# Expert layer in 512-token pairs, attention in 32-column tiles, and a written-out step order in a linear-attention and expert kernel

## The chip, the core and the metric

One core of a Trainium2 chip. TensorE multiplies matrices, VectorE and ScalarE do element-wise work, GpSimd (POOL) does little here, and SyncE (SP) issues the transfers. Times are microseconds on the device. The metric is the time of one execution of the whole program; three runs are given, and one more execution was profiled.

## The reference, cut to what matters

```python
# q, k, v, a_re, a_im: (4 batches, 8 heads, 768 steps, 48)
mag = sqrt(a_re**2 + a_im**2);  a = (a_re, a_im) * min(mag, 0.999) / (mag + 1e-6)
for t in range(768):
    S_re, S_im = a_t * S  (complex) + outer(k_t, v_t) on the real part
    y_t = q_t @ S_re
x = y as 3072 tokens of 384            # 8 heads x 48
h = x @ w_in                           # 384 -> 2048
g = h * sigmoid(1.702 * h)
out = g @ w_out                        # 2048 -> 384
```

All data are float32. The recurrence is computed in blocks of 128 steps: running products of magnitudes and running sums of angles scale and rotate q and k, so that inside a block a masked product of q and k stands for the recurrence, and a 96-row state carries it from block to block. Each head has a cosine and a sine part, 2 x 48 rows.

## The kernel before, in words

**Units.** The 3072 tokens are cut into 12 units of T = 256 tokens, three to a batch, and each unit has two halves of 128. A unit passes through three stages.

*Preparation* (`prepare_part`, L512 to L644): the coefficients are loaded into `ri`, ScalarE takes squares, logarithms, exponentials, an arctangent and sines, VectorE multiplies, and runs three kinds of scan (L570, L586, L604) over 3 x 256 columns. Six buffers `s0` to `s5` hold what is between, and their roles rotate from unit to unit. q and k are scaled and rotated in `qk` and `qr` and then copied by SP (`remap`, L646) into `qkh`, head by head: the cosine part in rows 0 to 47, the sine part in rows 64 to 111, the gaps being zero from memsets at the start (L384 to L386). Unit 0 is prepared in two halves.

*Attention* (`attend`, L657): for each half and each group of four heads, `scores` (L690) multiplies k by q into the PSUM bank `p_ps` in column tiles 64 wide, VectorE multiplies by the mask into `pm` (L694), `mix` (L716) adds masked scores times v and the state times q into `x_ps` in tiles 32 wide, `turn` (L736) transposes k of 112 rows into the bank `k_ps`, ScalarE copies it to `kt` (L747), `zed` (L743) multiplies it by v into `z_ps` in tiles of 48 columns, and VectorE adds it to the state `st` (L752). ScalarE rounds `x_ps` into `xhi` (L724), VectorE puts the rest into `xlo` (L728).

*Expert layer* (`moe`, L761): for each of 8 blocks of 256 hidden columns, `hidden` (L782) multiplies weights by the unit's 256 tokens into one of two banks `h_ps`, ScalarE writes Silu in float32 into `g32` (L794), VectorE rounds it into `gh` (L796) and puts the rest into `gl` (L797), and `project` (L812) multiplies slices of `gh` and `gl` (128 tokens wide, stationary) by 384 columns of output weights (moving) into two banks `o_ps`. Each product of float32 values is three products of rounded ones: high by high, high by low, low by high. VectorE copies `o_ps` to `osb` (L823) and SP stores it (L826). Unit 0 uses whole float32 weights and activations, which takes TensorE two passes a matmul, because the split of the weights is not done yet. So a unit of 256 tokens has 144 hidden matmuls of 256 columns and 96 output matmuls of 384; unit 0 has 48 and 32.

**Weights** come as 64-bit words, are converted (`convert`, L446: L462 on ScalarE, L463, L466, L469 on VectorE) and split into high and low (`split`, L471), 16 pieces of each. `inspect` and `sign` read weights and coefficients again and reduce them (L839, L858); `decide` (L862) turns the result into a flag, and at the end the program takes a general path (`general`, L890) if the data were out of range, which they are not here. The opening matmuls (L637) come before the first scores.

**Order.** Every step is added to a `Plan` (L82) with its engine, an estimated duration, a rank, and what it reads and writes. `Plan.order` (L291) plays the steps forward and backward with these durations, 160 rounds for each of five settings, and keeps the order with the lowest estimated cost; the rank comes from `prep_rank`, `attn_rank`, `moe_rank` and so on (L1075 to L1096). The steps are issued in this order, so each engine's stream is fixed, and an engine waits at the first instruction that is not ready. SP's queue is one of these streams. ScalarE loads a set of functions (L999) where a step needs another one than the last.

Of the kernel before, what the change touches and what calls it, by code (L numbers as in the profile page):

```python
# [10 lines left out]
F32 = mybir.dt.float32  # L11
# [10 lines left out]
P = 128  # L22
L = 128
HL = 64
# [11 lines left out]
KD = 112  # L36
UPB = 3
TWO_PI = 6.2831845
# [18 lines left out]
class Clock:  # L57


    def __init__(self):  # L60
        self.now, self.done, self.full = -1, 0.0, False

    def end(self, start, dur, work):
        t = start
        while dur > 1e-6:
            k = int(t / WINDOW + 1e-9)
            if k != self.now:
                self.full = k == self.now + 1 and self.done >= BUSY
                self.now, self.done = k, 0.0
            rate = 1.0 if self.full else 0.5  # L70
            step = min(dur, ((k + 1) * WINDOW - t) * rate)
            self.done += step * work
            dur -= step
            t += step / rate
        return t


def lag(a, b):
    return LAG if b != "PE" else 0.0 if a == b else LAG_PE


class Plan:  # L82
# [5 lines left out]
    def add(self, eng, dur, rank, fn, r=(), w=(), tab=None, name="", grp=None, work=1.0):  # L88
# [9 lines left out]
        self.ops.append((eng, dur, rank, fn, deps, tab, name, grp, work))  # L98

    def link(self):  # L100
        self.after = [[] for _ in self.ops]
        for n, o in enumerate(self.ops):
            for d in o[4]:
                self.after[d].append(n)

    def groups(self):
        todo = {}
        for o in self.ops:
            if o[7] is not None:
                todo[o[7]] = todo.get(o[7], 0) + 1  # L110
        return todo

    def forward(self, rank):

        ops, after = self.ops, self.after
        left = [len(o[4]) for o in ops]
        ready = [0.0] * len(ops)
        free = dict(FREE)
        wait = {e: [] for e in ENGINES}
        can = {e: [] for e in ENGINES}  # L120
        table, hw, dma, idle = None, 0.0, 0.0, 0.7
        todo, held = self.groups(), None
        clock = Clock()
        for n, k in enumerate(left):
            if not k:
                heapq.heappush(wait[ops[n][0]], (0.0, n))
        start = [0.0] * len(ops)
        done = 0
        while done < len(ops):
            best = None  # L130
            for e in ENGINES:
                while wait[e] and wait[e][0][0] <= free[e]:
                    n = heapq.heappop(wait[e])[1]
                    heapq.heappush(can[e], (rank[n], n))
                if can[e]:
                    s = free[e]
                elif wait[e]:
                    s = wait[e][0][0]
                else:
                    continue  # L140
                if best is None or s < best[0]:
                    best = (s, e)
            s, e = best
            if not can[e]:
                while wait[e] and wait[e][0][0] <= s:
                    n = heapq.heappop(wait[e])[1]
                    heapq.heappush(can[e], (rank[n], n))
            if e == "ACT":
                fit = [x for x in can[e] if ops[x[1]][5] in (None, table) or held in (None, ops[x[1]][7])]
                if not fit:  # L150
                    later = [free[x] for x in ENGINES if x != e and free[x] > s]
                    later += [wait[e][0][0]] if wait[e] else []
# [1009 lines left out]
```

## Time and profile before

| what | value |
|---|---|
| median of three runs | 596.96 us (594.47 to 601.34) |
| the profiled execution, whole | 595.74 us |
| its span, first to last instruction | 594.3 us |
| granted TensorE clock, mean | 0.996 of full speed |
| TensorE / VectorE / ScalarE busy | 557.5 / 472.4 / 272.1 us |
| HBM read / written | 53.87 / 4.72 MB |

The span is the profiled execution without what lies around its first and last instruction, 1.44 us. A busy engine has an instruction in work; matmuls are pipelined, so the distance between their starts tells their price, and not the length of one.

### The profile page before, as it was taken

How to read it: one execution, taken by the hardware profiler on the slowest of the kernel's cores; microseconds unless marked ns; L12 is line 12 of the kernel's file. 1: busy time of each engine (PE TensorE's matmuls, PEld its weight loads, DVE VectorE, ACT ScalarE, POOL GpSimd, SP SyncE). 2: the span in 40 equal slices, each digit the busy share in tenths (PEclk: the TensorE clock that was granted, in tenths of full speed). 3: DMA queues.
4: the chain of work that ended last, by engine and by line, in shares of the span. 5: the costliest groups of instructions: out<-in, count | busy, mean ns of one | idle time of the engine just before them, and what ended most of it. 6: DMA issues, size and time to landing. Idle time of an engine off the chain costs nothing.

```text
span 594.3 us, 13835 instructions
## 1 busy us (share of the span) xinstructions
PE 557.5 (94%) x5804; PEld 512.9 (86%) x5804; DVE 472.4 (79%) x827; ACT 272.1 (46%) x373; POOL 23.8 (4%) x75
## 2 busy tenths in 40 slices
PE   0489999999999999899999999999899999999995
PEld 0377778999989999899999899999889999999994
DVE  7999999989879788788789697798689779554433
ACT  8878477247463552742732723532552642111110
POOL 5110000000010000000000000000000000000000
PEclk9999999999999999999999999999999999999998
DMA  8478962363651830833807825743851832722211
GB/s 344 143 257 333 236 191 70 73 143 129 108 168 32 175 120 14 163 108 84 191 33 130 230 80 110 174 149 92 156 185 47 205 93 64 168 73 58 68 43 41
DMA packets 31526, 78.48 MB, mean 132 GB/s; under 512 B 4448, under 2 KB 9568, under 8 KB 31456
## 3 DMA queue, kind: packets, MB, share of 16 engines
q1 hardware_dynamic: 31456, 77.52, 48.6%
q8 instruction: 47, 0.77, 0.6%
q14 instruction: 23, 0.19, 0.1%
HBM read 53.87 MB, written 4.72 MB: 99 GB/s over the span
## 4 chain that ended last, share of the span: by engine, by line
PE 86%; DMA 4%; ACT 3%; DVE 3%; SPq 1%; issue 0%; ACTq 0%
PE o_ps L812 34%; PE h_ps L782 33%; PE x_ps L716 7%; PE p_ps L690 6%; PE z_ps L743 3%; PE k_ps L736 3%; DMA qkh<-qk 2%; DMA raw<-in_w_out_dram 1%; PE h_ps L637 1%; DMA raw_w<-in_w_in_dram 1%; DVE qk L444 1%; DMA ri<-in_a_dram 1%; DVE pm L694 1%; ACT L999 0%; ACT raw L462 0%; DVE s L604 0%
## 5 line engine op out<-in xcount | busy, mean ns | idle before, releaser
L782 PE MATMUL h_ps<-xhi,hiA 128*128 128x256 f32 x528 | 152.0, 288 | 0.0
L782 PE MATMUL h_ps<-xlo,hiA 128*128 128x256 f32 x528 | 149.0, 282 | 0.0
L782 PE MATMUL h_ps<-xhi,loA 128*128 128x256 f32 x528 | 149.0, 282 | 0.0
L794 ACT ACTIVATE g<-h_ps 128x512 f32<-128x512 f32 x88 | 52.7, 598 | 173.5 <-PE h_ps L782 99.6
L782 PEld LDWEIGHTS h_ps<-xhi,hiA 128*128 128x128 f32 x528 | 100.2, 190 | 2.4 <-issue 1.2
L782 PEld LDWEIGHTS h_ps<-xlo,hiA 128*128 128x128 f32 x528 | 100.3, 190 | 0.3
L782 PEld LDWEIGHTS h_ps<-xhi,loA 128*128 128x128 f32 x528 | 100.5, 190 | 0.0
L812 PE MATMUL o_ps<-hiU,gh 128*128 128x384 f32 x352 | 93.9, 347 | 0.0
L812 PE MATMUL o_ps<-loU,gh 128*128 128x384 f32 x352 | 89.7, 335 | 0.0
L812 PE MATMUL o_ps<-hiU,gl 128*128 128x384 f32 x352 | 89.6, 335 | 0.0
L812 PEld LDWEIGHTS o_ps<-loU,gh 128*128 128x128 f32 x352 | 63.7, 188 | 0.0
L812 PEld LDWEIGHTS o_ps<-hiU,gl 128*128 128x128 f32 x352 | 63.6, 188 | 0.0
L797 DVE TENSOR_TENSOR gl<-g,gh 128x512 fp32r<-128x512 f32 x88 | 60.4, 687 | 3.7
L796 DVE CAST gh<-g 128x512 fp32r<-128x512 f32 x88 | 36.9, 419 | 31.3 <-ACT g L794 21.1
L812 PEld LDWEIGHTS o_ps<-hiU,gh 128*128 128x128 f32 x352 | 57.6, 190 | 3.9 <-issue 2.6
L839 DVE TENSOR_REDUCE fit<-raw_w 128x1 f32<-128x256 f32 x96 | 37.6, 411 | 19.1 <-DMA raw_w<-in_w_in_dram 9.7
L690 PEld LDWEIGHTS p_ps<-qkh 128*64 128x64 f32 x768 | 36.9, 136 | 13.7 <-issue 4.6
L694 DVE TENSOR_TENSOR pm<-p_ps,mask 128x512 f32<-128x512 f32 x48 | 32.9, 686 | 19.7 <-PE p_ps L690 19.4
L690 PE MATMUL p_ps<-qkh 128*64 128x128 f32 (+1 forms) x768 | 43.6, 253 | 4.5 <-DMA qkh<-qk 2.6
L444 DVE TENSOR_TENSOR qk<-qk,s 128x768 f32<-128x768 f32 (+1 forms) x52 | 45.6, 889 | 2.5 <-ACT s L630 2.2
L999 ACT ACT_TABLE_LOAD x36 | 46.2, 1283 | 1.4 <-PEq L1150 0.8
L747 ACT ACTIVATE kt<-k_ps 128x448 f32<-128x448 f32 x40 | 21.7, 543 | 41.4 <-PE k_ps L736 25.5
(94 smaller groups left out, 763.8 us busy)
## 6 DMA issues: line engine op xcount, KB each, us to landing
v<-in_v_dram SPq DMA_DIRECT2D x24, 352.0 KB, 3.8
ri<-in_a_dram SPq DMA_DIRECT2D x11, 768.0 KB, 5.2
qk<-in_qk_dram SPq DMA_DIRECT2D x11, 768.0 KB, 4.9
qkh<-qr SPq DMA_DIRECT2D x22, 288.6 KB, 5.9
qkh<-qk SPq DMA_DIRECT2D x22, 288.6 KB, 6.5
raw<-in_w_in_dram SPq DMA_DIRECT2D x8, 768.0 KB, 7.3
raw<-in_w_out_dram SPq DMA_DIRECT2D x8, 768.0 KB, 6.6
raw_w<-in_w_in_dram SPq DMA_DIRECT2D x24, 256.0 KB, 2.8
```

The costliest lines, as they stand in the source:

```text
L444: add(en, t, rank, lambda: e.tensor_tensor(out=out, in0=a, in1=b, op=alu), **kw)
L690: mm(p_ps[to : to + HL, j, lo:L], lhsT=at(h, 1, c)[:, lo : lo + HL], rhs=at(h, 0, c)[:, lo:L], start=True, stop=True)
L694: add("DVE", d_t(CW), rk(4 * c + hh), lambda hh=hh: dve.tensor_tensor(out=pm[hh].rearrange("p (a b) t -> p a b t", b=2), in0=p_ps.rearrang ...
L716: mm(x_ps[32 * j : 32 * j + 32, r, :], lhsT=lt, rhs=rt, start=n == 0, stop=n == len(steps) - 1)
L747: add("ACT", a_t(4 * KD) - 0.12, rk(4 * c + hh), lambda: act(out=kt[0][:, :, 0:KD], in_=k_ps[:, :, 0:KD], func=AF.Copy), r=["K"], w=["kt"])
L782: mm(h_ps[hb][:, f, :], lhsT=ww[:, r * T + f * P : r * T + (f + 1) * P], rhs=x[:, r, :], start=n == 0, stop=n == last)
L794: add("ACT", a_t(CW) - 0.15, rk(i), lambda hb=hb: act(out=g32, in_=h_ps[hb], func=AF.Silu, scale=SLOPE), r=[f"h{hb}"], w=["g"], tab=SILU, ...
L796: add("DVE", d_t(CW, 2), rk(i), lambda gb=gb: dve.tensor_copy(out=high.g(gb), in_=g32), r=["g"], w=[f"gh{gb}"])
L797: add("DVE", d_t(CW), rk(i), lambda gb=gb: dve.tensor_tensor(out=glo[gb], in0=g32, in1=high.g(gb).bitcast(F32), op=ALU.subtract), r=["g", ...
L812: mm(o_ps[t], lhsT=x[:, f, t * L : (t + 1) * L], rhs=y[:, f * DM : (f + 1) * DM], start=i == 0 and f == 0 and n == 0, stop=i == NP - 1 and ...
L839: add("DVE", d_t(CK), rk + 2, lambda x=x, op=op: dve.tensor_reduce(out=f_w[:, x, n : n + 1], in_=weights.looked_at()[:, :, 1], op=op, axis ...
L999: nc.scalar.preload_act_table_set(o[5])
```

## The change

1. **Pairs.** `GROUPS` makes one expert layer of units 4 and 5, one of 6 and 7, 8 and 9, 10 and 11. It has 512 tokens: hidden matmuls of 512 columns, 16 steps of 128 hidden columns. Units 0 to 3 stay alone. `xhi`, `xlo` hold 512 tokens.
2. **Output transposed.** `project` has the weights stationary and the activations moving, 256 or 512 columns, into three banks `o_ps` (128 output columns each); the output is stored transposed and turned on the host. A single unit has 144 output matmuls of 256 columns, a pair 144 of 512; unit 0 has 48 of 256.
3. **Rounded activation.** ScalarE runs Silu twice on the hidden bank: once into `gh`, rounded, and once in place. VectorE subtracts from the bank into `gl`. `g32` and the rounding copy go.
4. **96 rows.** The sine part of q and k is in rows 48 to 95; the memsets of `qkh` go, and transposes have 96 columns.
5. **32-column tiles.** Scores are 16 matmuls in tiles 32 wide with 128, 96, 64 and 32 moving columns; `mask` has four parts; `v` comes with copies rolled by 32, 64 and 96 rows. `zed` is one step for eight heads with tiles of 32. Transposes go to the bank of the scores (unit 0: also to banks of the output).
6. **Attention order.** The x block and state of a half are added after the scores of the next half's first four heads, except in unit 0 and at the end of a group.
7. **Buffers.** Five slots instead of six: the scan of L586 writes over its input.
8. **Step order.** The planner goes; `ORDER` lists the 1864 steps by the number in which the code adds them. It has the form that the planner returned.

```diff
+GROUPS = ((0,), (1,), (2,), (3,), (4, 5), (6, 7), (8, 9), (10, 11))
+PAIR = 2 * T
-KD = 112
+KD = 96
...
     def order(self):
-        (planner: forward, backward, time, 5 x 160 rounds)
+        order = [int(x) for x in ORDER.split()]
+        place = {n: k for k, n in enumerate(order)}
+        assert len(order) == len(place) == len(self.ops)
+        assert all(place[d] < place[n] for n, o in enumerate(self.ops) for d in o[4])
+        return order
...
-                    out=w(qm)[:, r, :], data0=m[:, r, :], data1=c[:, r, :],
+                    out=c[:, r, :], data0=m[:, r, :], data1=c[:, r, :],
...
-        dst = qkh[hb_(u)][64 * x : 64 * x + D, ...]
+        dst = qkh[hb_(u)][D * x : D * x + D, ...]
...
+            def scores(hh, c=c, bank=bank):
+                ps_ = bank("P", hh)[0]
+                for x in range(4):
                     for j in range(4):
+                        h, lo = 4 * hh + j, QL * x
+                        to = QL * ((x + j) % 4)
+                        mm(ps_[to : to + QL, j, lo:L], lhsT=at(h, 1, c)[:, lo : lo + QL], rhs=at(h, 0, c)[:, lo:L],
+                           start=True, stop=True)
...
+                    for h in range(H):
                         lo = h * VP + h % 2 * (VP - D)
+                        for g in range(KD // QL):
+                            mm(z_ps[g * QL : (g + 1) * QL, lo : lo + D], lhsT=kt[h // 4][:, h % 4, g * QL : (g + 1) * QL],
                                rhs=vt[:, lo : lo + D], start=True, stop=True)
...
+            if waiting:
+                o_blend, o_state, o_out, o_update, o_skip, o_reads = waiting.pop()
+                o_blend((0, 2), grp, [*hk[c], *o_reads["z"]])
+                score(0, (), grp)
+                o_blend((1,), grp)
+                o_out()
+                if not o_skip:
+                    o_state(grp)
+                    o_update()
...
+                score(1, (), grp)
...
-                add("ACT", ..., act(out=g32, in_=h_ps[hb], func=AF.Silu, scale=SLOPE), ...)
-                add("DVE", ..., dve.tensor_copy(out=high.g(gb), in_=g32), ...)
-                add("DVE", ..., dve.tensor_tensor(out=glo[gb], in0=g32, in1=high.g(gb).bitcast(F32), op=ALU.subtract), ...)
+                add("ACT", ..., act(out=high.g(gb), in_=h_ps[hb], func=AF.Silu, scale=SLOPE), ...)
+                add("ACT", ..., act(out=h_ps[hb], in_=h_ps[hb], func=AF.Silu, scale=SLOPE), ...)
+                add("DVE", ..., dve.tensor_tensor(out=glo[gb], in0=h_ps[hb], in1=high.g(gb).bitcast(F32), op=ALU.subtract), ...)
...
-                        mm(o_ps[t], lhsT=x[:, f, t * L : (t + 1) * L], rhs=y[:, f * DM : (f + 1) * DM], ...)
+                    mm(o_ps[c][:, 0:n_t], lhsT=y[:, f * DM + c * P : f * DM + (c + 1) * P], rhs=x[:, k * n_t : (k + 1) * n_t], ...)
...
+        for u in us:
+            prepare(u)
+            attend(u)
+        moe(g)
...
+ORDER = """
+80 130 0 10 185 169 101 151 15 81 82 83 132 131 84 133 85 89 86 134 2 135 93 3
...
+1684 1681 1685 1686 1682 1687 1689 1690 1688 1694 1691 1692 1695 1862 1863 1693
+"""
```

## Rows read from the trace of the kernel before

**Rows 1.** The page's first part: busy time, share of the span and number of instructions of each engine.

```profile
PE 557.5 (94%) x5804; PEld 512.9 (86%) x5804; DVE 472.4 (79%) x827; ACT 272.1 (46%) x373; POOL 23.8 (4%) x75
```

**Rows 2.** The table of five stretches of the span, cut where TensorE starts, where unit 1's output is copied, where unit 4's expert layer starts and where TensorE ends. Behind the stretch stand its length, then busy time and number of instructions of each engine, the granted TensorE clock, the DMA share and the GB/s.

```profile
0.00:22.64 22.64, 0.00 (x0) 0.03 (x1) 19.22 (x49) 19.29 (x34) 8.23 (x18) 1.00 0.74 279
22.64:146.00 123.36, 120.92 (x1208) 100.70 (x1209) 118.81 (x181) 79.38 (x106) 6.87 (x17) 1.00 0.61 178
146.00:236.50 90.50, 90.50 (x974) 86.41 (x973) 75.60 (x126) 42.70 (x57) 2.27 (x10) 1.00 0.43 104
236.50:587.10 350.60, 346.04 (x3627) 325.81 (x3626) 258.24 (x475) 130.73 (x178) 6.41 (x30) 1.00 0.46 115
587.10:594.30 7.20, 0.00 (x0) 0.00 (x0) 0.50 (x2) 0.00 (x0) 0.00 (x0) 0.69 0.20 67
```

**Rows 3.** Who waited for whom over the whole span: total in us, times, the longest.

```profile
ACT g L794 <- PE h_ps L782: 99.6, 37, 7.4
...
PE p_ps L690 <- DMA qkh<-qk: 2.6, 2, 1.8
...
PE o_ps L812 <- ACT g L790: 0.7, 1, 0.7
```

**Rows 4.** The chain of work in order of time, two stretches: start us, us, what. Unit 0's blocks, in which each fp32 matmul appears as two passes, and unit 1's.

```profile
51.79 2.59 PE h_ps L782 x12
54.38 2.58 PE o_ps L812 x8
...
99.18 5.39 PE h_ps L782 x45
...
107.89 2.08 PE o_ps L812 x12
```

**Rows 5.** TensorE's timeline in two stretches with attention of unit 1: start us, us from the first start to the last end, line, tiles, shape of the stationary and the moving operand, number of instructions. An fp32 matmul is two instructions.

```profile
82.66 1.56 PE L782 MATMUL h_ps<-x,valA 128*128 128x256 f32 x6
84.15 0.43 PE L716 MATMUL x_ps<-pm,v 128*32 128x128 f32 x8
84.39 0.40 PE L716 MATMUL x_ps<-qkh,st 128*32 128x128 f32 x8
...
85.27 0.40 PE L716 MATMUL x_ps<-qkh,st 128*32 128x128 f32 x8
85.60 0.89 PE L690 MATMUL p_ps<-qkh 128*64 128x128 f32 x16
86.32 0.53 PE L743 MATMUL z_ps<-v,kt 128*48 128x48 f32 x16
86.78 0.60 PE L736 MATMUL k_ps<-ident,qkh 112*128 112x112 f32 x4
87.22 0.50 PE L812 MATMUL o_ps<-valU,g 128*128 128x384 f32 x1
...
93.48 0.56 PE L743 MATMUL z_ps<-v,kt 128*48 128x48 f32 x16
93.98 0.38 PE L782 MATMUL h_ps<-xhi,hiA 128*128 128x256 f32 x1
```

**Rows 6.** Groups of instructions over the whole span, shapes kept apart: line, engine, operation, out<-in, shapes, count | busy us, mean ns of one | idle of the engine just before them, and what ended it.

```profile
L797 DVE TENSOR_TENSOR gl<-g,gh 128x512 fp32r<-128x512 f32 x88 | 60.4, 687 | 3.7
...
L794 ACT ACTIVATE g<-h_ps 128x512 f32<-128x512 f32 x88 | 52.7, 598 | 173.5 <-PE h_ps L782 99.6 <-DVE gl L797 58.3 <-PE o_ps L812 6.3
L999 ACT ACT_TABLE_LOAD x36 | 46.2, 1283 | 1.4 <-PEq L1150 0.8
L444 DVE TENSOR_TENSOR qk<-qk,s 128x768 f32<-128x768 f32 x44 | 41.3, 952 | 2.4 <-ACT s L630 2.2
...
L796 DVE CAST gh<-g 128x512 fp32r<-128x512 f32 x88 | 36.9, 419 | 31.3 <-ACT g L794 21.1 <-PE o_ps L812 10.1
L694 DVE TENSOR_TENSOR pm<-p_ps,mask 128x512 f32<-128x512 f32 x48 | 32.9, 686 | 19.7 <-PE p_ps L690 19.4
...
L743 PE MATMUL z_ps<-v,kt 128*48 128x48 f32 x640 | 22.4, 212 | 0.0
...
L586 DVE TENSOR_TENSOR_SCAN s<-s,small,s 128x256 f32<-128x256 f32 x33 | 22.3, 729 | 0.0
...
L728 DVE TENSOR_TENSOR xlo<-x_ps,xhi 128x384 fp32r<-128x384 f32 x22 | 12.1, 552 | 4.8 <-ACT xhi L724 4.7
...
L752 DVE TENSOR_TENSOR st<-z_ps,st 128x448 f32<-128x448 f32 x16 | 9.9, 618 | 5.0 <-PE z_ps L743 5.0
...
L637 PE MATMUL h_ps<-qk,ident 128*128 128x256 f32 x26 | 7.8, 471 | 22.6 <-DVE qk L444 22.6
L469 DVE CUSTOM_DVE_ANT_0 valA<-raw,valA 128x1536 uint16<-128x1536 uint16 x8 | 7.6, 951 | 0.0
...
L560 DVE TENSOR_SCALAR s<-s 128x768 f32<-128x768 f32 x11 | 7.6, 689 | 0.4
L466 DVE SCALAR_TENSOR_TENSOR valA<-raw,valA 128x768 int32<-128x768 int32 x8 | 7.6, 946 | 0.0
...
L487 DVE TENSOR_TENSOR loA<-valA,hiA 128x768 fp32r<-128x768 f32 x8 | 7.5, 941 | 0.0
...
L463 DVE TENSOR_SCALAR valA<-raw 128x768 int32<-128x768 int32 x8 | 4.6, 574 | 0.0
...
L384 DVE MEMSET qkh<- 128x2048 f32 x1 | 1.8, 1765 | 0.4 <-issue 0.4
```

More of the change, by code (lines that the diff above doesn't have):

```diff
@@ L54 @@
 SLOPE = 1.702
[L57 to L79, printed above, removed]
 class Plan:
@@ L291, in order @@
-    def order(self):
-        self.link()
-        best = None
-        for part in PARTS:
-            rank = [o[2] for o in self.ops]
-            for k in range(ROUNDS):
-                start, end = self.forward(rank)
-                order = sorted(range(len(start)), key=lambda n: start[n])
-                cost = sum(w * self.time(order, x) for x, w in COST)
-                if best is None or cost < best[0]:
-                    best = (cost, order)
-                late = self.backward(start)
-                rank = [x + part * (end - y - x) for x, y in zip(rank, late)]
-        return best[1]
@@ L655, in remap @@
             dma(out=dst[E0:D, 2 * NR + j, :], in_=src[2 * D + j * rest : 2 * D + (j + 1) * rest, 1, :])
+    blocks, waiting = [0], []
     def attend(u):
@@ new lines, in attend, with blend @@
+            reads = {
+                "x": [kv, *hk[c], "pm0", "pm1"] + ([f"st{src}"] if have else []),
+                "z": [] if skip else [kv, "kt0", "kt1"],
+            }
+            def blend(rs, grp=None, also=(), c=c, mix=mix, have=have, reads=reads):
+                for r in rs:
+                    add("PE", (0.44 if r < 2 else 0.88) * (1 if have else 0.5), rk(4 * c + 2), lambda r=r: mix(r),
+                        r=[*(x for x in reads["x"] if r == 2 or x != f"pm{1 - r}"), *also], w=["x"], work=0.72, cols=E0)
@@ L765, in moe @@
+            if not skip:
+                keys(0)
+                keys(1)
+            if u == 0 or ends and c == 1:
+                finish()
+            else:
+                waiting.append((blend, state, out_of, update, skip, reads))
+    def moe(g):
+        us = GROUPS[g]
+        u, b, n_t = us[0], g % 2, T * len(us)
+        whole = g == 0
+        xk = [f"x{y}{b}.{c}" for y in ("h" if whole else "hl") for c in range(2 * len(us))]
         both_halves = "v" if whole else "hl"
+        per = CW // n_t
+        n_s = 2 * NP // per
@@ L767, in rk, with t_mm, hidden @@
         def rk(s):
-            return moe_rank(u, s)
-        for i in range(NP):
-            hb = (NP * u + i) % 2
-            def hidden(f, i=i, hb=hb):
+            return moe_rank(u, s * 8 * len(us) / n_s)
+        def t_mm(n):
+            return n * 4 / 2400 + 0.004 if whole else (n + 32) / 2400
+        for s in range(n_s):
+            hb = gb = s % 2
+            fs = [divmod(s * per + k, 2) for k in range(per)]
+            def hidden(k, fs=fs, hb=hb):
+                i, f = fs[k]
@@ L781, in hidden @@
                     for ww, x in terms:
[L782 removed]
+                        mm(h_ps[hb][:, k * n_t : (k + 1) * n_t], lhsT=ww[:, r * T + f * P : r * T + (f + 1) * P],
+                           rhs=x[:, r, 0:n_t], start=n == 0, stop=n == last)
                         n += 1
[L785 to L787 removed]
@@ L1053, in high, with place @@
         return self.tile(f"hi{m}{i // 2}", f"h{m}{i // 2}", [P, 2, WC], F32R)[:, i % 2, :]
+GROUP_OF = {u: n for n, g in enumerate(GROUPS) for u in g}
+def place(u):
+    n = GROUP_OF[u]
+    if n == 0:
+        return -8.0, 8.0
+    own, before = GROUPS[n], GROUPS[n - 1]
+    width = 8.0 * len(before) / len(own)
+    return 8.0 * before[0] + own.index(u) * width, width
 STAGE = {
```

521 lines of the change are left out of this document (170 added, 351 removed), and 76 rows, old and new, of the table ORDER.

## The prediction

> **What bounds the kernel now.** I read the page's shares first. TensorE is busy 94% of the span, VectorE 79%, ScalarE 46% [rows 1]. A share says nothing about stages, so the table of stretches came next [rows 2]; the granted clock in it is full speed until TensorE's end. Until 22.64 us TensorE does nothing. From there to 146 us it is busy 120.92 of 123.36 us and VectorE 118.81: both are full. From 146 to 236.5 us TensorE has no idle time and VectorE 14.9 us of it. From 236.5 to 587.1 us TensorE is idle 4.6 us. The last 7.2 us hold a store and the program's end. The table of waits says the same from the other side: after the first 22.6 us TensorE's own waits are a few of 2.6 us or less in sum, while ScalarE waits 99.6 us for hidden blocks to be done [rows 3]. So TensorE's stream of instructions sets the time after 22.6 us, with VectorE just behind it in the first 146 us.
>
> Busy is not the same as streaming, so I priced the stream. In the chain, 45 hidden matmuls of 256 columns take 5.39 us (119.8 ns each), 12 output matmuls of 384 columns 2.08 us (173.3 ns), and in unit 0, where fp32 makes two passes of each matmul, 12 passes of 256 columns take 2.59 us (215.8 ns) and 8 of 384 take 2.58 us (322.5 ns) [rows 4]. In the attention, eight 32-column instructions follow each other in 0.22 us, so a round of four takes 0.109 us for 128 moving columns; 16 score instructions take 0.72 us including a start of 0.055 us, that is 0.664; 16 state instructions take 0.36 us and 0.10 to leave, in pairs of 0.045 us; four transposes of 112 columns take 0.384 us and 0.055 to start [rows 5]. The sum: unit 0, 96 x 0.2158 + 64 x 0.3225 = 41.4; eleven units x (144 x 0.1198 + 96 x 0.1733 = 33.9) = 372.8; scores 48 x 0.664 = 31.9; transposes 160 x 0.096 = 15.4; states 320 pairs x 0.045 = 14.4; x blocks 1408/4 x 0.109 = 38.4; the opening matmuls 7.8 [rows 6]. Together 522.1 us of 557.5 busy. The other 35 us are changes of tile width: from a 128-column hidden block to a 32-column one 82.66 to 84.15 us is 1.49 us for six passes worth 1.295, so 0.19 us; the way back costs 0.14 us (93.48 to 93.98 for a state block worth 0.36); 32 to 64 columns costs 0.11 to 0.14 us (85.27 to 85.60 for 0.22) [rows 5].
>
> **The change, part by part, on TensorE.** *Pairs of units.* A 512-column matmul is in no row. The step from 256 to 384 columns is 53.5 ns, so the next one gives 226.8 ns. From below the nearest row is 215.8 ns, a pass that streams 512 fp32 words' worth; from above twice the 256-column one, 239.6. I take 226.8, since two rows lie on its line. The eight paired units cost 8 x 33.9 = 271.1 us now and 4 x 288 x 0.2268 = 261.3 then: -9.8, with bounds of -22.5 and +4.9. Units 1 to 3 turn 96 output matmuls of 384 into 144 of 256: +0.6 each, +1.8. Unit 0: +0.1. *Scores in 32-column tiles.* Sixteen matmuls in four widths; rounds of four by the rows above and a straight line between them take 0.109, 0.083, 0.057 and 0.031 us, twice each: 0.56 against 0.664, 48 times, -5.0. *96 rows.* Transposes of 96 columns: 4 x 14 ns less, 40 times, -2.2. The state matmuls keep 16 rounds of 48 columns (three tiles abreast, not two): 0. The x blocks: 0. *Step order.* I numbered the steps as the code adds them and read TensorE's part of the table: it goes from 128-column work (hidden, output, transposes) to 32-column work (scores, x, states) 38 times, and back 38 times; nothing is 64 wide any more. 38 x (0.19 + 0.14) = 12.5 us instead of 35: -22.5. All of it: -37.6 us. If TensorE alone set the time, 595.7 would become 558.
>
> **What is late next.** VectorE loses the rounding copy (36.9 us), and a 1.8 us memset, and gains little [rows 6]: 434 us in all. But a pair needs both units' attention before its first hidden block, so work moves forward. In the table 309 VectorE steps stand up to the last input of the first paired hidden block (unit 5's second half): weights 64 steps, preparation of units 0 to 6 in full, attention of 0 to 5, 24 subtractions, 9 output copies, 12 inspections. With each row's mean less 0.06 us for the overlap of neighbours (the 827 durations add to 522 us, busy is 472.4) that is: weights 16 x 3.16 = 50.6; unit 0 in its 32 half-size steps 17.9; units 1 to 6, of which a late one has 13 steps x 0.89, 3 x 0.63, 9 scans of about 0.65 and 0.4 of small ones = 19.6 and the first three hand some to ScalarE, 15.7 + 17.2 + 19.0 + 3 x 19.6 = 110.7; two steps of unit 7, 1.8; attention 24 x 0.63 + 10 x 0.49 + 15 x 0.56 = 28.3; subtractions 24 x 0.63 = 15.0; 3.2 and 4.2 for the last two. Together 232 us [rows 6]; the same sum over all steps gives 439 for 434, so 229. VectorE's idle time up to then: it was 8.0 us by 146 us, 3.4 of it before 22.64 [rows 2]; carried on at that rate it is 11.4 by 240. I take 9.7. So the first paired block starts at 239 us. TensorE by itself would be there at 22.64 + 196.9 (its steps before it) + 2.2 (opening matmuls at their row) + 23 x 0.33 + 2.4 idle as now = 232. VectorE is 7 us later, and takes that much of the gain.
>
> After it TensorE has 261.3 (pairs) + 24 x 0.56 + 20 x 0.33 + 10 x 0.72 + 704/4 x 0.109 = 307.7, 15 x 0.33 = 5.0 for widths, 4.6 idle as now, 7.2 for the end: 239 + 324.5 = 563.5 us of span. The profiled execution lasts 595.74 for a span of 594.3, so 565 us; it lies 1.2 under the median shown, and I leave that inside the range.
>
> *ScalarE.* The second Silu per hidden block adds 88 x 0.6 = 52.7 us; the table changes function sets 58 times, not 36, +22 x 1.28 = 28.2 [rows 6]. 272 becomes 351, 62% of the span; cover is the 99.6 us in which it now waits for TensorE. An in-place Silu on PSUM is in no row; the nearest is the one into SBUF, 598 ns, which I take. At nothing ScalarE would have 299 us of work, at twice the price 404, and either is under the span, so the price is felt only where ScalarE is late (C). The subtraction reads PSUM instead of SBUF: the mask product on the same shape from PSUM takes 686 ns, this one 687, so 0. New waits: the next hidden block but one waits for the subtraction, not for the first Silu, so its bank is held some 1.4 us longer (0.6 + 0.69 and a hand-over); behind it on TensorE stand the output blocks, and what covers it is the hidden block between (2.0 us) and two thirds of an output block (1.4). Transposes share a bank with the scores and wait for the mask product (0.69 us); the table mostly puts 1 to 2 us of hidden or output work between them. The x block of a half also waits for the q/k of the next half, with scores and all expert work behind it. Setup: VectorE's 1.8 us memset and two on GpSimd go, but VectorE has 3.4 us idle before 22.64 anyway [rows 2], so 0. SP issues in the table's order too: a late q/k transfer shows as TensorE waiting on it, 2.6 us now [rows 3], inside the 4.6, and the four pair starts are where more of it would stand.
> The Trainium skill ("ScalarE: Activation LUTs", What ACT_TABLE_LOAD costs) gives 2.66 us for a switch, drain included. By it the 22 would cost 58 us. The trace has 1283 ns a load and 1.4 us of idle time before all 36 together [rows 6], so I count no drain.
>
> **Rivals.** *A. TensorE alone bounds* (chance 0.20): the VectorE work up to 239 us is hidden better than I sum it. For: now VectorE has 14.9 us idle between 146 and 236.5. Against: that is because TensorE was slower. Time: 232 + 324.5 + 1.4 = 558.
> *B. Small matmuls are bound by issue* (0.10). The state rows start 22.5 ns apart; I read this as 48 columns streaming, but it may be a floor. Then scores are 32 x 22.5 = 0.72 us and states 48 x 22.5 = 1.08: +0.16 and +0.36 each, after 239 us 24 x 0.16 + 10 x 0.36 = 7.4 us; before it VectorE hides them. Against: x instructions on different tiles follow within one round of four. Time 572.
> The Trainium skill ("TensorE: Matmul & The Clock Gate", Wait — 56ns, not 53.3ns?) states such a floor: starts never closer than about 25 ns. By it B costs 10.6 us and gives 576. The state rows, at (0.53 - 0.21)/15 = 21 ns apart [rows 5, 6], already pass under it, which is why B has a small chance.
> *C. ScalarE in the fixed order makes TensorE wait, and the kernel is slower* (0.04). Between two Silu pairs the table has eight stretches of 7.2 to 11.7 us of other ScalarE work and loads, 73 us together. If TensorE had only the next hidden block (2.0 us) beside each, 57 us would be lost: 622 us. It ends above 597 once 32 of these 57 are lost, 4 us a stretch. Against: TensorE waits 0.7 us for a Silu in the whole trace of before, though the same preparation groups stand there [rows 3].
> The forecast itself has 0.60, mostly within 559 to 571; 0.06 is for what I have not thought of.
>
> **How the numbers follow.** The range reaches from A with a cheaper 512-column matmul (565 - 13 = 552) to the forecast with the dear one (565 + 14 = 579) and a little more, 581; B lies inside. About 1% (6 us) is what a measurement of this kernel can tell from no change. Faster by over 1% is everything but C and part of the unknown: 0.95; within 1%: 0.03; slower: 0.02.
>
> **What would show it.** Paired hidden and output matmuls start 226.8 ns apart; a score block takes 0.56 us and its neighbours of 32 columns follow without a gap; TensorE's busy time is near 520 us; VectorE's near 434; 58 table loads. The first paired hidden block starts near 239 us, TensorE has some 12 us of idle time between 23 and 239 us, with VectorE as what ended it, and less than 6 after. I am wrong if TensorE is idle more than 10 us after the first pair, if ScalarE's Silu ends its waits, or if the widths still cost over 20 us.

## The result, and the profile after

The changed kernel takes 580.19 us (median of four, 576.9 to 588.92), the kernel before 596.68 beside it: a ratio of 0.9695 [0.9613, 0.9777] (it compares means without the longest execution, whose granted clock was 0.980 against 0.989 and 0.990 in the others, and so lies below the quotient of the medians). The forecast was 565 with a range of 552 to 581, so the time lies at the upper end of the range, 15 us above the forecast. The profiled execution lasted 580.61 us for a span of 578.9.

The page after, shares of the busy engines, and further down the queue of TensorE's instructions (packets, MB, share):

```profile
PE 531.9 (92%) x6300; PEld 461.0 (80%) x6300; DVE 435.6 (75%) x739; ACT 337.6 (58%) x483; POOL 23.9 (4%) x83
...
q8 instruction: 51, 0.84, 0.6%
```

The changed kernel's stretches, with the columns of [rows 2], cut where TensorE starts, at 146 and 236.5 us as before, where the first paired hidden block starts, and where TensorE ends:

```profile
0.00:23.79 23.79, 0.00 (x1) 0.03 (x1) 18.45 (x51) 18.74 (x32) 5.96 (x26) 1.00 0.73 273
23.79:146.00 122.21, 112.91 (x1490) 98.83 (x1491) 113.94 (x169) 88.90 (x120) 7.88 (x16) 0.97 0.56 175
146.00:236.50 90.50, 86.41 (x1306) 84.37 (x1305) 86.22 (x136) 61.53 (x84) 3.63 (x16) 0.98 0.57 154
236.50:253.30 16.80, 15.70 (x324) 15.08 (x323) 10.68 (x20) 9.63 (x15) 0.00 (x0) 1.00 0.36 72
253.30:571.80 318.50, 316.88 (x3188) 262.70 (x3186) 205.64 (x366) 158.76 (x236) 6.42 (x25) 1.00 0.40 114
```

Read the first busy column (TensorE) and the clock. Behind 253.3 us TensorE is idle 1.6 us in 318.5. Ahead of it, from its start at 23.79, it is idle 122.21 - 112.91 + 90.50 - 86.41 + 16.80 - 15.70 = 14.5 us, and its granted clock is .97 and .98, where before it was 1.00 and TensorE full [rows 2]. VectorE (third busy column) has done 18.45 + 113.94 + 86.22 + 10.68 = 229.3 us of work by 253.3 us, and so was idle 24.0.

TensorE's own waits in the changed kernel behind its start, those of 0.7 us or more (total in us, times, longest):

```profile
PE p_ps L484 <- issue: 5.9, 5, 2.6
PE z_ps L521 <- ACT kt L502: 2.4, 1, 2.4
PE x_ps L469 <- DVE pm L490: 1.6, 1, 1.6
PE x_ps L469 <- ACT x L527: 1.3, 1, 1.3
PE o_ps L645 <- issue: 1.3, 2, 0.7
PE p_ps L499 <- ACT kt L502: 1.0, 1, 1.0
PE o_ps L645 <- DVE valU L232: 0.7, 1, 0.7
```

The longest sum is "issue": the score blocks (L484) stop in their middle, and the view names no engine, buffer or transfer that they wait for. The timeline of TensorE shows the worst one, and what comes behind it (three dots stand for rows left out):

```profile
227.25 0.85 PE L521 MATMUL z_ps<-v,kt 128*32 128x48 f32 x48
227.93 0.85 PE L484 MATMUL p_ps<-qkh 96*32 96x128 f32 x29
231.37 0.32 PE L484 MATMUL p_ps<-qkh 96*32 96x32 f32 x3 [2.59 <-issue]
231.62 1.01 PE L645 MATMUL o_ps<-gl,hiU 128*128 128x256 f32 x3
232.43 0.41 PE L615 MATMUL h_ps<-xhi,hiA 128*128 128x256 f32 x1
232.64 0.41 PE L615 MATMUL h_ps<-xlo,hiA 128*128 128x256 f32 x1
...
234.91 0.28 PE L615 MATMUL h_ps<-xhi,hiA 128*128 128x256 f32 x1
235.03 0.28 PE L615 MATMUL h_ps<-xlo,hiA 128*128 128x256 f32 x1
```

After 29 of the block's 32 instructions TensorE stands for 2.59 us. Behind the stop the 256-column matmuls start 0.21 us apart, then 0.12 as in the chain of before [rows 4]: the clock fell to the lower of its two levels (1.2 GHz; granted 0.50 from 231.4 us) after the idle time and rose again at about 234.8 us. It did the same at 43.7 to 50.5 us, behind the stops that begin at 40.4 and 43.7 us in unit 0.

The groups that answer to [rows 6]:

```profile
L615 PE MATMUL h_ps<-xhi,hiA 128*128 128x512 f32 x192 | 75.7, 394 | 0.0
...
L841 ACT ACT_TABLE_LOAD x58 | 74.4, 1283 | 1.8 <-PEq L1091 0.8
...
L632 DVE TENSOR_TENSOR gl<-h_ps,gh 128x512 fp32r<-128x512 f32 x88 | 60.0, 685 | 55.5 <-ACT h_ps L630 50.0 <-PE o_ps L645 3.3 <-issue 2.0
...
L628 ACT ACTIVATE gh<-h_ps 128x512 fp32r<-128x512 f32 x88 | 52.4, 597 | 136.0 <-PE h_ps L615 96.5 <-PE o_ps L645 39.1
L630 ACT ACTIVATE h_ps<-h_ps 128x512 f32<-128x512 f32 x88 | 51.8, 593 | 0.0
```

The prices of the added operations came out as taken: the second Silu 593 ns, the subtraction from PSUM 685, 58 loads at 1283. A few lines of the paired part show the stream:

```profile
443.27 0.43 PE L469 MATMUL x_ps<-pm,v 128*32 128x128 f32 x8
443.51 0.41 PE L469 MATMUL x_ps<-qkh,st 96*32 96x128 f32 x8
443.73 0.74 PE L484 MATMUL p_ps<-qkh 96*32 96x128 f32 x32
444.29 0.40 PE L469 MATMUL x_ps<-pm,v 128*32 128x128 f32 x8
...
447.76 0.40 PE L615 MATMUL h_ps<-xhi,hiA 128*128 128x512 f32 x1
447.99 0.39 PE L615 MATMUL h_ps<-xlo,hiA 128*128 128x512 f32 x1
448.22 0.39 PE L615 MATMUL h_ps<-xhi,loA 128*128 128x512 f32 x1
```

A score block lasts 444.29 - 443.73 = 0.56 us and its neighbours follow without a gap; 512-column matmuls start 0.23 us apart.

### The profile page after: what moved, and what is told of

Same layout as the page of the kernel before. It is cut to its first block, busy times and chain, and to the rows that moved or that the text cites. A ratio compares the mean times of both kernels' runs of the same rounds, so it can differ in the third digit from the quotient of the medians.

```text
span 578.9 us, 14799 instructions
## 1 busy us (share of the span) xinstructions
PE 531.9 (92%) x6300; PEld 461.0 (80%) x6300; DVE 435.6 (75%) x739; ACT 337.6 (58%) x483; POOL 23.9 (4%) x83
## 4 chain that ended last, share of the span: by engine, by line
PE 63%; DVE 3%; issue 1%; DMA 1%; ACT 1%; SPq 0%; DVEq 0%
PE o_ps L645 26%; PE h_ps L615 25%; PE x_ps L469 5%; PE p_ps L484 4%; PE p_ps L499 1%; PE z_ps L521 1%; DMA out_dram<-osb 1%; DVE qk L207 1%; DVE osb L661 0%; DVE qr L207 0%; DVE s L207 0%; DVE s L333 0%; DVE pm L490 0%; DVE gl L632 0%; ACT s L319 0%
## 5 line engine op out<-in xcount | busy, mean ns | idle before, releaser
L615 PE MATMUL h_ps<-xhi,hiA 128*128 128x512 f32 (+1 forms) x336 | 117.8, 351 | 0.3 <-DVE gl L632 0.3
L615 PE MATMUL h_ps<-xlo,hiA 128*128 128x512 f32 (+1 forms) x336 | 116.1, 345 | 0.0
L615 PE MATMUL h_ps<-xhi,loA 128*128 128x512 f32 (+1 forms) x336 | 116.0, 345 | 0.0
L632 DVE TENSOR_TENSOR gl<-h_ps,gh 128x512 fp32r<-128x512 f32 x88 | 60.0, 685 | 55.5 <-ACT h_ps L630 50.0
L645 PE MATMUL o_ps<-gl,hiU 128*128 128x512 f32 (+1 forms) x336 | 85.5, 353 | 1.3 <-issue 1.3
L645 PE MATMUL o_ps<-gh,hiU 128*128 128x512 f32 (+1 forms) x336 | 84.6, 351 | 0.0
L645 PE MATMUL o_ps<-gh,loU 128*128 128x512 f32 (+1 forms) x336 | 82.4, 344 | 0.0
L841 ACT ACT_TABLE_LOAD x58 | 74.4, 1283 | 1.8 <-PEq L1091 0.8
L645 PEld LDWEIGHTS o_ps<-gl,hiU 128*128 128x128 f32 x336 | 56.6, 191 | 9.4 <-issue 2.1
L645 PEld LDWEIGHTS o_ps<-gh,loU 128*128 128x128 f32 x336 | 57.6, 189 | 7.8
L645 PEld LDWEIGHTS o_ps<-gh,hiU 128*128 128x128 f32 x336 | 56.6, 189 | 7.5 <-issue 0.4
L484 PEld LDWEIGHTS p_ps<-qkh 96*32 96x32 f32 x1472 | 33.4, 109 | 13.8 <-issue 10.6
L484 PE MATMUL p_ps<-qkh 96*32 96x128 f32 (+3 forms) x1472 | 38.1, 235 | 6.5 <-issue 5.9
```

What stands on the lines that cost most here:

```text
L484: mm(ps_[to : to + QL, j, lo:L], lhsT=at(h, 1, c)[:, lo : lo + QL], rhs=at(h, 0, c)[:, lo:L], start=True, stop=True)
L615: mm(h_ps[hb][:, k * n_t : (k + 1) * n_t], lhsT=ww[:, r * T + f * P : r * T + (f + 1) * P], rhs=x[:, r, 0:n_t], start=n == 0, stop=n == last)
L632: add("DVE", d_t(CW), rk(s), lambda hb=hb, gb=gb: dve.tensor_tensor(out=glo[gb], in0=h_ps[hb], in1=high.g(gb).bitcast(F32), op=ALU.subtrac ...
L645: mm(o_ps[c][:, 0:n_t], lhsT=y[:, f * DM + c * P : f * DM + (c + 1) * P], rhs=x[:, k * n_t : (k + 1) * n_t], start=i == 0 and f == 0 and n ...
L841: nc.scalar.preload_act_table_set(o[5])
```

## The experiments

Theories: V, VectorE's amount of work sets the start of the first pair (the prediction's step); I, TensorE stops for its own instructions in the dense attention blocks; F (later T, C, D for its pieces), single late inputs in the first 90 us stop TensorE. Times are medians; ratios are to the kernel before on the same chip.

**e1_kt_first.** Edit: in the table, ScalarE's copy of weight block 4 (21) later, behind the copies of the transposed keys (191, 193), its rounding of unit 0's first x block (181) earlier, right behind them, and VectorE's two mask products (187, 189) earlier.

```diff
-... 188 303 35 30 180 190 21 192 191 193 22 304 189 198 23 290 181 187 ...
+... 188 35 30 180 187 189 303 190 192 191 193 181 22 304 21 198 23 290 ...
```

> The changed kernel with six steps of its table moved: in unit 0's second half ScalarE copies the transposed keys and rounds the first half's x before it copies the weight piece whose load is late, and VectorE makes the two mask products before a scan. Theory F (waits in the first 60 us are on the path): the gaps of 1.6, 2.4 and 1.3 us on TensorE between 33 and 45 us shrink to under 2 us in sum, the half clock of 6.8 us behind them goes, the first paired hidden block starts 5 to 8 us earlier than 253.3, time 572 to 576. Theory V (the amount of VectorE work up to the first pair paces): VectorE's work is the same, so the first paired block moves by under 2 us and the time stays at 578 to 581.

Measured: 584.5 us, 0.9795 [0.974, 0.985]. The wait for the keys fell from 2.4 to 0.3 us, but TensorE then waited 5.8 us for weights at 68.5 us, and the issue stops of the score blocks came to 7.1 us (5.9 in the changed kernel), behind the same instructions of TensorE's stream as in the changed kernel (the 1451st, 5522nd, 6033rd, 7305th, 7813th, loads counted). The time is above the range of either theory. Moving one late input gave nothing; the stops did not care about the waits ahead of them.

**e2_shift.** Edit:

```diff
+    for k in range(32):
+        nc.tensor.matmul(h_ps[1][0:32, 0:1], lhsT=ident[:, 0:32], rhs=ident[:, 0:1], start=True, stop=True)
```

> The changed kernel with 32 one-column fp32 matmuls on the identity ahead of everything, while TensorE has nothing else to do: 128 more TensorE instructions, no other work. Theory I (TensorE's stops in the middle of a score or x block are waits for instructions, which come 256 at a time): the stops stand at other instructions, 128 earlier or later in the code; the one of 2.6 us at 228.6 us goes or moves, time within 4 us of 580, either way. Rival (they are waits for data or for a bank): the same instructions wait, the 2.6 us stop stays, time 579 to 581.

Measured: 573.25 us, 0.9616 [0.958, 0.9653]: more instructions, and less time by 7 us in the medians, 5 by the ratios. No score block stops any more (one issue wait of 0.5 us is left, in an x block). In this trace the wait for weights near 70 us, 0.7 us in the changed kernel's, is 5 us, with the clock's fall behind it (an fp32 output instruction every 0.22 us ahead of it, every 0.45 behind it; lines of this run and of the later ones with a new start stand 3 higher):

```profile
65.75 3.40 PE L648 MATMUL o_ps<-g,valU 128*128 128x256 f32 x15
68.99 1.46 PE L618 MATMUL h_ps<-x,valA 128*128 128x256 f32 x6
75.46 2.90 PE L648 MATMUL o_ps<-g,valU 128*128 128x256 f32 x6 [5.01 <-DVE valU L235]
```

**e5_shift256.** Edit: `range(64)` in place of `range(32)`.

> 64 one-column fp32 matmuls at the start in place of the 32 of the run e2_shift: 256 more TensorE instructions (a fp32 matmul is two loads and two matmuls), so one whole instruction packet of the trace, and every later instruction keeps its place within its packet as in the changed kernel. Theory I (the stops in score blocks are waits for the next packet of instructions, set by where its border falls): the stops come back in the same blocks as in the changed kernel (near 90, 214, 229, 246, 301 and 338 us, 0.5 to 2.6 us each, about 6 us in sum), 577 to 583 us. Rival H (the run e2_shift was faster because TensorE had work in its first 20 us, or by chance): no stops of over 0.5 us named issue, 570 to 575 us.

Measured: 583.2 us, 0.975 [0.9707, 0.9792]. The profiled execution took 589.84 us, so only the places are read from it: the stops are back at 95.8, 218.2, 232.3, 249.5, 309.4, 330.3 and 347.5 us, in the same blocks, and the worst block again after 29 of 32:

```profile
231.46 0.85 PE L487 MATMUL p_ps<-qkh 96*32 96x128 f32 x29
234.79 0.32 PE L487 MATMUL p_ps<-qkh 96*32 96x32 f32 x3 [2.47 <-issue]
```

The last instructions ahead of the seven stops are the 1707th, 5272nd, 5778th, 6289th, 7561st, 8069th and 8577th of TensorE's stream: each 256 later than in the changed kernel, to the instruction. Theory I holds, H falls.

**e3_planner and e4_singles.** Edits: the planner of the kernel before in place of the table; and beside it no pairs.

```diff
+        (planner: forward, backward, time, 5 x 160 rounds)
-        order = [int(x) for x in ORDER.split()]
...
-GROUPS = ((0,), (1,), (2,), (3,), (4, 5), (6, 7), (8, 9), (10, 11))
+GROUPS = tuple((u,) for u in range(12))
```

> The changed kernel with the planner of the kernel before in place of the table (same steps, same estimated durations in the code). If the table is worth what its few width changes give (38 times each way against the planner's likely 70 or more, at 0.33 us): 585 to 592, with VectorE's idle time before the first pair much the same. If the order is worth little, 578 to 582. Faster than 577 would say that the table itself costs time.

> The same as with the planner, but every unit alone, no pairs: expert matmuls of 256 columns only. By the sum on TensorE the pairs give 8 x 144 x 2 x 0.1198 - 4 x 288 x 0.2268 = 14.8 us, so this should be 10 to 15 us slower than the run with the planner and pairs. Rival: pairs need two units' attention ahead, which makes TensorE wait in the first half, so that without them only 0 to 5 us are lost.

Measured: 600.65 us, 1.0092 [1.0056, 1.0128], and 617.46, 1.0382. With everything of the change but its order the kernel is 0.9% slower than before, and slower than the 585 to 592 us expected. The page's shares of e3_planner:

```profile
PE 544.0 (91%) x6300; PEld 461.1 (77%) x6300; DVE 439.2 (73%) x739; ACT 317.6 (53%) x466; POOL 21.3 (4%) x83
```

and of e4_singles, with its instruction queue:

```profile
PE 556.5 (90%) x7452; PEld 528.9 (86%) x7452; DVE 443.5 (72%) x751; ACT 321.8 (52%) x469; POOL 21.2 (3%) x83
...
q8 instruction: 60, 0.98, 0.7%
```

The table is worth 20.5 us (24 by the ratios). TensorE changes between 32 and 128 columns 145 times in e3's trace and 77 in the changed kernel's: 68 x 0.165 = 11.2 us by the prediction's price, and busy differs by 12.1 (13.8 with the slow clock of both traces, 3.4 and 5.1 us, taken out); the rest is idle time. The pairs are worth 16.8 us here, a little over the 10 to 15 expected; the same prices give 8 x (33.9 + 0.6) - 261.3 = 14.7. The packets of the instruction queue go with TensorE's instructions: 60 here, 51 in the changed kernel, 47 in the kernel before with its 2 x 5804.

**e6_less_dve.** Edit:

```diff
+        ct = (lambda q: q[:, :, 0:1]) if 3 <= u <= 6 else (lambda q: q)
-        both("sum", u, i, rk("sum"), m, m, d, ALU.add, ...)
+        both("sum", u, i, rk("sum"), ct(m), ct(m), ct(d), ALU.add, ...)
...
+        (the same in "ratio", "scq", "sck")
```

> In units 3 to 6 four VectorE steps each (the sum of squares, the ratio, the scaling of q and of k) work on 3 columns instead of 768 and so leave out that part of the preparation; every step keeps its place and its waits. It takes 16 x 0.88 = 14 us of VectorE work away ahead of the first paired hidden block, and adds and removes no TensorE instruction. Theory V (VectorE's amount of work sets the start of the first pair, as the prediction had it): the first pair starts 8 to 14 us earlier than 253 us, 566 to 573 us. Theory T (TensorE's own stream with its stops sets that start; VectorE's 24 us of idle time is what is left over): the first pair starts at 250 to 253 us, VectorE's idle time ahead of it grows to 35 to 38 us, 577 to 581 us.

Measured: 581.45 us, 0.9718 [0.965, 0.9787]. Its stretch up to the first pair:

```profile
0.00:251.20 251.20, 215.60 (x3114) 199.32 (x3115) 217.53 (x373) 178.67 (x248) 15.73 (x58) 0.97 0.57 171
```

VectorE did 217.5 us of work, 11.8 less, and was idle 33.7; the pair started 2.1 us earlier and the time did not move. This trace has a stop of 5.2 us for weights near 69 us that the changed kernel's has not, so the pair's start alone is not a clean comparison; but in the changed kernel VectorE ended only 3.3 of TensorE's 14.5 us of waits. V falls, and e9 below, where TensorE is idle only 3.6 us ahead of the pair, confirms it.

**e7_scores64.** Edit:

```diff
-                for x in range(4):
+                for x in range(2):
-                        h, lo = 4 * hh + j, QL * x
-                        to = QL * ((x + j) % 4)
+                        h, lo = 4 * hh + j, 64 * x
+                        to = 64 * ((x + j) % 2)
```

> The score blocks go back to tiles of 64 columns: 8 matmuls in place of 16 per block (so 16 x 48 = 768 matmuls fewer), all else as in the changed kernel; the rows of some heads' scores then stand in other places than the value rows, so that part is computed on other pairs. Theory W (the prediction's prices: 0.56 against 0.664 us a block, and 0.11 to 0.14 us for each change between 32 and 64 columns): a score block takes 0.66 us and the steps next to it 0.11 to 0.14 us more, 48 x 0.104 + 80 to 90 changes x 0.125 = 15 to 16 us more of TensorE's stream; fewer instructions take away the stops of about 6 us: 585 to 592 us. Rival N (what counts is the number of instructions, the widths cost nothing): 572 to 576 us.

Measured: 581.44 us, 0.9739 [0.9682, 0.9797], between the ranges of both and no different from the changed kernel. No issue stop is left (5.9 us in the changed kernel), but scores last longer. So the narrow tiles would have saved in stream what their doubled instructions gave back in stops. e11 separates the two.

**e8_fill.** Edit: 11 matmuls at the start, as in e2_shift, and in three places of the table

```diff
+    for k_ in (6, 10, 5):
+        add("PE", 0.2 * k_, 0, lambda k_=k_: [
+            mm(h_ps[1][:, 0:P], lhsT=ident, rhs=ident, start=True, stop=True) for x in range(k_)
+        ])
...
-... 178 ... 198 ... 194 ...
+... 1864 178 ... 1865 198 ... 1866 194 ...
```

> As the run e2_shift (128 more TensorE instructions), but 21 of the 32 extra matmuls are 128 columns wide and stand where TensorE waited in the first 46 us: 6 ahead of the wait at 33.9 us, 10 ahead of the one at 40.4, 5 ahead of the one at 43.7; 11 one-column ones stay at the start. Theory C (the stretch of half clock at 44 to 51 us follows these stops, and costs half its length): no half clock in 30 to 60 us, the first pair 3 to 4 us earlier than in e2_shift, 568 to 571 us. Rival K (the half clock is not due to these stops, or the time it costs is covered by VectorE further on): 572 to 575 us.

Measured: 574.31 us (569.54 to 576.07), 0.9605 [0.9545, 0.9666]: by its times no different from e2_shift, which is rival K's range. In the trace the clock is full to 71 us and the first pair starts at 248.5 us, not 251.5, as theory C had it; e12 decides between them. TensorE still stops 4.6 us at 68.1. What that stop waits for, SP's queue and VectorE's timeline say:

```profile
61.48 0.33 SPq L226 DMA_DIRECT2D raw<-in_w_out_dram  x1
61.91 1.18 SPq L418 DMA_DIRECT2D qkh<-qr  x2
63.13 0.76 SPq L419 DMA_DIRECT2D qkh<-qr  x1
...
71.13 0.56 DVE L229 TENSOR_SCALAR valU<-raw 128x768 int32<-128x768 int32 x1 [4.42 <-DMA raw<-in_w_out_dram]
```

The load of weight block 10 is issued at 61.48 us, when VectorE has freed its buffer, and right behind it come unit 1's q/k copies in small pieces. VectorE's first step on it starts 9.6 us after the issue. In the changed kernel's trace this wait was 0.9 us on VectorE and 0.7 on TensorE, in the six other traces with the table and no moved load (e1, e2, e5 to e8) 3.5 to 5.8 on TensorE.

**e9_all and e10_load.** Edit to e8_fill, and to the changed kernel: VectorE's steps 33 and 34 (block 6) ahead of the q/k scaling of unit 1, step 50 (the load) ahead of step 55.

```diff
-299 45 ... 55 337 33 203 311 204 34 312 47 50
+299 33 34 45 ... 50 55 337 203 311 204 312 47
```

> As the run e8_fill, and VectorE's two last steps on weight block 6 stand ahead of the scaling of unit 1's q and k in the table, so that their buffer is free 5 us earlier, and the load of block 10 stands one place earlier on SP's queue: it is issued at 56 to 57 us in place of 61.5, ahead of the q/k copies that are issued from 61.9 us. Theory D (the stop of 3.5 to 5.8 us near 68 us in six of the seven traces of this table, and the half clock of 6.83 us behind it, come from this load landing late among those copies): VectorE's step on block 10 waits for nothing, no stop of over 1 us and no half clock in 60 to 90 us, the first paired hidden block starts 6 to 9 us earlier than in e8_fill (at 240 to 243 us), 565 to 569 us. Rival V (VectorE's amount of work sets that start once TensorE's stops are gone): at most 3 us earlier, 571 to 574 us.

> The changed kernel with the load of weight block 10 and VectorE's two steps ahead of it moved alone, without the extra TensorE instructions and without the filled waits. Theory D with I: the stop near 69 us stays under 1 us in every execution, so the spread of the changed kernel's times (576.9 to 588.9) narrows to its lower end, 575 to 579 us; the stops named issue stay, about 6 us, and the half clock at 44 us too. Rival V: no change, 579 to 582 us.

Measured: e9_all 568.04 us (567.11 to 572.1), 0.9531 [0.9493, 0.9568], the fastest of all; e10_load 578.5 (575.86 to 581.65), 0.9688 [0.9651, 0.9724]. In e9_all the load is issued at 56.39 us and VectorE waits for nothing:

```profile
56.39 0.33 SPq L226 DMA_DIRECT2D raw<-in_w_out_dram  x1
...
65.91 0.55 DVE L229 TENSOR_SCALAR valU<-raw 128x768 int32<-128x768 int32 x1
```

Its stretches, cut at TensorE's first real matmul, 146 us, the first pair and TensorE's end:

```profile
0.00:22.90 22.90, 1.33 (x22) 1.25 (x22) 18.32 (x50) 18.44 (x32) 6.00 (x26) 1.00 0.75 282
22.90:146.00 123.10, 120.44 (x1570) 106.78 (x1571) 118.60 (x176) 93.87 (x126) 7.73 (x16) 1.00 0.56 177
146.00:242.30 96.30, 95.35 (x1590) 93.08 (x1589) 92.64 (x150) 67.19 (x93) 3.60 (x16) 1.00 0.58 155
242.30:558.60 316.30, 315.79 (x3188) 262.45 (x3186) 204.92 (x365) 158.03 (x235) 6.72 (x25) 1.00 0.41 114
```

TensorE is idle 3.6 us ahead of the pair, the clock is full, and the pair starts at 242.3 us; VectorE did the same 229.6 us of work, with 12.7 idle. The stop and the slow clock behind it are gone, as D had it, for 6.3 us against e8 (4.4 by the ratios). Why the load was late is not separated: from issue to landing it took 8.9 to 10.9 us in the six traces, but 6.1 in the changed kernel's with the same copies behind it, and 5.4 to 8.6 in e10 to e12 (e9's landing is not in the trace). What is shown is that an earlier issue takes the wait away. Alone (e10_load) the move is not told apart from the changed kernel by the intervals, though the spread is narrower; its trace has the wait at 68 us gone, the issue stops (7.7 us) and the slow clock at 43 us as ever.

**e12_shift_load.** Edit: the two moves of e9_all on e2_shift, without the filled waits.

> The run e2_shift with the load of weight block 10 and VectorE's two steps ahead of it moved as in e9_all, but without the filled waits: TensorE's stops at 33.7, 40.1 and 43.5 us (5 us in sum) and the half clock of 6.83 us behind them stay. Theory C (these waits and the clock after them are on the path): the first paired hidden block starts 3 to 4 us later than in e9_all, at 245 to 247 us, 570 to 573 us. Rival K (they are covered further on): 566 to 569 us, as e9_all.

Measured: 572.38 us, 0.9607 [0.9577, 0.9637]; in its trace the pair starts at 245.8 us with TensorE idle 9.4 from 23.8, and the slow clock is back at 44 us. Theory C holds: the waits in unit 0 and the clock behind them are on the path, for about 4 us (4.3 in the medians, 4.5 by the ratios).

**e11_all_scores64.** Edit: that of e7_scores64 on e9_all.

> The run e9_all with the score blocks in tiles of 64 columns, as in e7_scores64 (768 matmuls fewer; some heads' scores are placed in other rows, so that part is computed on other pairs). In e9_all no stop over 0.6 us is left for fewer instructions to take away, so this shows the price of the wider tiles alone. By the blocks of e7_scores64 (from a block's start to the next one's: scores 37.6 us in 46 blocks, in e9_all 31.6; the blocks next to them 44.6 + 17.6 against 41.3 + 14.4, of which 3 us are front waits) it is 6 + 3.5 = 9 to 10 us: theory W, 575 to 579 us. By the prediction's prices it would be 15 to 16 us: 583 to 585 us. Rival N (widths cost nothing, the number of instructions alone counts): 566 to 569 us.

Measured: 575.65 us, 0.9669 [0.9653, 0.9686]: 7.6 us more than e9_all (8.2 by the ratios), though TensorE has no issue stop and 1536 instructions fewer. Theory W holds. My expectation counted the changes of width wrongly: the trace has 46 between 32 and 64 columns, not 80 to 90, so the prediction's prices give 48 x 0.104 + 46 x 0.125 = 10.7 us, not 15 to 16. TensorE's busy time grew by 10.1 us (543.0 on this run's page, 532.9 on e9's), near that price; the time grew by less, since TensorE is idle 0.9 us in this trace and 4.0 in e9's, from its start on.

## Why the prediction was right, and which step was off

*The stream, right.* The 512-column matmul at 0.227 us, the score block at 0.56, the second Silu, the subtraction, 58 loads, and VectorE's work of 229 us ahead of the pair (229.3) came out as priced. Behind the first pair the sum was 307.7 + 5.0 + 4.6 = 317.3 us; measured 318.5, though with 1.6 idle, not 4.6, so the stream there is 4.2 us longer than its price. The change takes its gain where the prediction put it: pairs (e4 against e3) and the fewer width changes of the table (e3 against the changed kernel). TensorE's busy time is 531.9, not near 520: 5 us are the slow clock, and 7 are stream priced too low, 4.2 of them behind the pair; which operation it is was not settled. The widths cost about what was taken (e3's 12.1 against 11.2 us, e11's 10.1 us of busy time against 10.7), and changes are 77, where 76 were counted in the table. Off without weight: ScalarE's 272 + 52.7 + 28.2 is 353, not 351, and busy is 337.6, because the sum left out that neighbours overlap.

*The step that failed: the start of the first pair.* The prediction had it as VectorE's 229 us of work plus 9.7 us of idle time, carried on from the trace of before (at that rate it would be 11.4; why 9.7 was taken is not said): 239 us. It was 253.3, with 24.0 idle. The size of the idle time was wrong because its cause was: it is not VectorE that sets this start. With 11.8 us of VectorE's work gone the pair starts 2.1 us earlier and the time stays (e6). It is TensorE, which the prediction had at 232 with 2.4 idle. Add what the trace has: its start 1.15 later, 14.5 - 2.4 = 12.1 of stops, and 5.1 for 10.2 us at half the clock, and 232 becomes 250.4; 2.9 of 253.3 are left for the stream. VectorE waits behind TensorE, and its idle time is what that leaves. So the mechanism of rival A (TensorE alone bounds) is the one that the runs show, and its 558 lacked the stops: 558 + 1.15 + 12.1 + 5.1 for them, 2.9 for the stream ahead of the pair and 1.2 behind it make 580.5. That 580 lies inside the range at all is luck: the upper end stood for a dearer 512-column matmul, which came out at its price, and neither the forecast nor a rival had these stops.

*What the stops are.* The prediction let TensorE's idle time go on as before, and expected VectorE to end it. Three kinds came instead. (1) Issue stops, 7.2 us in all, one with a slow clock behind it: all but 0.5 us removed by moving every instruction by half a packet (e2, 5 to 7 us less), restored by moving it by a whole one (e5). (2) Waits of unit 0 for keys and x: worth 4 us with the clock behind them (e12 against e9). (3) A weight load that lands late: 0.7 us in this trace, 3.5 to 5.8 in most others, worth 4 to 6 us (e8 against e9). With nearly all of them removed (e9), the pair starts at 242.3 us and the kernel takes 568.0.

*Rivals.* B fell: 32 score instructions in 0.56 us are 17.5 ns apart, and 48 state instructions in 0.68 us (227.25 to 227.93) are 14. What small instructions did cost is a wait for the next packet, which B did not have. The Trainium skill ("TensorE: Matmul & The Clock Gate", Wait — 56ns, not 53.3ns?) has starts never closer than about 25 ns; on four tiles abreast this trace has them closer. C fell: ScalarE ends 4.7 us of TensorE's waits, and all of it for keys and x, none for a Silu. The Trainium skill ("ScalarE: Activation LUTs", What ACT_TABLE_LOAD costs) gives 2.66 us a switch with its drain; here 58 loads took 1283 ns each with 1.8 us of idle time ahead of all, so by these rows the drain is not seen.

*Where the stops stand.* The traces tell more of the issue stops than the experiments asked. With TensorE's semaphore instructions counted too, the changed kernel's seven stand behind its first 1473, 5057, 5569, 6081, 7361, 7873 and 8385 recorded instructions: 193 and a multiple of 256 each time. So do all other issue stops behind the first 43 recorded instructions in every run's trace, the 0.5 us that is left in e2 among them (6337). And each ends 1.2 to 1.9 us after a packet of the instruction queue has landed. Inside the worst stop, from 228.78 to 231.37 us, the queue's count is

```profile
q8 instruction: 1, 0.02, 2.5%
```

and that packet ran from 228.91 to 229.96 us. So TensorE stood at a packet's border and waited for a packet that came late.

*What stays open.* Why a packet is fetched late is not settled: in the seven places its transfer began 0.8 to 3.1 us after TensorE had passed the border before, and the 256 instructions in between, without the stop, ran in 2.9 to 4.5 us; in slower code the same delay did no harm, and in other dense stretches the packet came in time. Other phases than half and whole packets were not tried.

## What to carry to other kernels

Price an engine's stream and its stops apart, and do not carry idle time over from a kernel whose order is replaced: ask which engine's idle time is only what another's stops leave. Halving tiles doubles instructions, and a dense run of small ones can wait for instructions themselves: look for "issue" in the middle of a block, and move the whole stream by a few dummy instructions to test it. Ahead of a stretch that is full on two engines a single late load costs twice, once as idle time and again in the slower clock behind it.

## What the runs showed of the hardware

TensorE's instructions come in packets of 16 KB; the number of packets goes with that of its instructions (12,690 recorded ones and 51 packets, 45 packets in e7, 60 in e4), and the stops stand 256 recorded instructions, or a multiple of it, apart. Where 256 instructions passed in 2.9 to 4.5 us and the next packet was late, TensorE stopped for up to 2.59 us, mostly in attention blocks, and went on 1.2 to 1.9 us after the packet had landed. It did so behind the same few instructions in every trace with the same stream (the 5522nd, 6033rd and 7305th in the changed kernel, e1, e6 and e10), and 128 more instructions at the start took nearly all the stops away. The same number of matmuls is thus not the same time.

Each idle stretch of 2 to 5.8 us behind TensorE's first 25 us was followed by its lower clock, in every trace (256-column matmuls 0.21 us apart in place of 0.12, fp32 ones 0.45 in place of 0.22); of shorter ones some were and some were not. Filled with useless matmuls, the idle time of unit 0 left the clock full there (e8, e9).
